# First key chunk ahead: the opening of an attention and SwiGLU kernel loaded and ordered anew

## The chip, the cores and the metric

The kernel runs on one core of one Trainium2 chip. The metric is the device time of one execution in microseconds (us), lower is better. The engines are called by the names that the profile uses: PE (TensorE, matrix products), ACT (ScalarE, functions), DVE (VectorE, elementwise work), POOL (GpSimd, here issues loads and copies) and SP (SyncE, issues DMAs). PEld is PE's loading of weights.

## The reference

Attention over 8 batches of 12 heads, 448 tokens and 64 dimensions, and behind it a gated feed-forward block (SwiGLU) over 3584 tokens, 768 wide inside and 1536 in the middle. All inputs come as float32.

```python
scores = scale * np.matmul(q, k.transpose(0, 1, 3, 2))      # q, k, v: 8, 12, 448, 64
attn = np.exp(scores - max); attn = attn / (sum(attn) + 1e-09)
x = np.matmul(attn, v)                                      # -> 3584 x 768
g = x @ w_gate
out = (g * sigmoid(g)) * (x @ w_val) @ w_out                # -> 3584 x 768
```

## The kernel before

The kernel works in fp16 with float32 accumulation. Heads are taken in pairs: pair 0 to 5 make batch 0, and there are 48 pairs in all. A pair's 448 keys are cut in four chunks (`NC`) of 112 (`P`). The work on a pair has these steps, and the letters are those of the order written out by hand in `OPENING`:

- **T** (`prep(pr)()`, function `turn`, lines 293 to 303): queries and keys of a pair are turned by 18 small matmuls against an identity (line 302) and copied by DVE (line 303) into `qkT`: columns 0 to 447 the keys, the rest the queries, the first 64 columns of them twice.
- **S** (`qk(pr, c)`, lines 353 to 367): two matmuls, one for each head, score a chunk of keys against all queries (line 359); ACT takes the exponential into `E` (line 367). The stationary operand has 128 columns, so it reads 16 columns of the next chunk along.
- **C** (`copy_v`, line 218): DVE copies the loaded values into a tile with a column of ones.
- **P** (`pv_chunk`, lines 377 to 411): eight matmuls (lines 385 and 393) multiply a chunk of exponentials with the values. After a pair's fourth chunk DVE divides by the sums (lines 404 and 406).
- **X** (`turn_x`, line 485): the pair's result is turned by three matmuls and DVE copies it (line 492) into `X`, the input of the feed-forward block.
- **D** (`dummy(1)`, line 163): one matmul of 512 columns on a tile of zeros, whose result nothing reads.

Each engine takes its instructions in the order in which the program emits them, so `OPENING` is the order of PE through the six pairs of batch 0, of ACT's exponentials, and of DVE's copies. After it a plan interleaves later pairs with the feed-forward steps; the first of them starts with the gate matmuls (`gp`, line 557) of batch 0, needs the X of pairs 0 to 4 at once and that of pair 5 a little later. In what follows S2.0 is chunk 0 of pair 2, and T6 the turn of pair 6.

Scores, turns and several later steps share a ring of three score buffers in PSUM (`ps_s`): a step that takes one waits until the work on the third one before it is done, an exponential for a score or a copy for a turn.

Loads: pair 0 is loaded by SP in float32 (`load_qk32`), one DMA for its queries and one for its keys. It is cast by DVE and ACT, one head each, turned by 16 matmuls (`turn0`, line 278) and copied by both (lines 286 to 289). All other pairs, the values and the weights are loaded by POOL's queue, which turns them to fp16 on the way (`load_qk16`, line 200; `load_v`, line 211; from pair 12 on also line 177). The first of these loads stand in a list before `OPENING`; later ones are emitted beside the second score chunk of a pair, from the table `wq`. From pair 11 on turns are done by POOL copies and DMA transposes issued by SP, no longer by PE.

Of the kernel before, what the change touches and what calls it, by code (L numbers as in the profile page):

```python
# [10 lines left out]
FP32 = mybir.dt.float32  # L11
FP16 = mybir.dt.float16
AF = mybir.ActivationFunctionType
# [5 lines left out]
GP = 3  # L19
NPE = 11  # L20
# [8 lines left out]
QB = 5  # L29
# [35 lines left out]
def kernel(  # L65
# [10 lines left out]
    nc = tc.nc  # L76
    B, H, S, D = q.shape
    DM = H * D
    DF = moe_w_gate.shape[1]
    P = 112  # L80
    NC = S // P
# [27 lines left out]
    attp = ctx.enter_context(tc.tile_pool(name="attp", bufs=4))  # L109
# [46 lines left out]
    raw = {}  # L156
# [3 lines left out]
    def dummy(n, w=4):  # L160
        wp = ps_f.tile([128, 512], FP32, tag="f", name="wp")
        for _ in range(n):
            nc.tensor.matmul(wp[:, 0 : w * 128], lhsT=warm[:], rhs=warm4[:, 0:w], start=True, stop=True)

    def load_qk32(pr):
        rq = fp.tile([P, 2, NC, D], FP32, tag="osb", bufs=4, name="rq")
        rk = fp.tile([P, 2, NC, D], FP32, tag="osb", bufs=4, name="rk")
        for dst, src in ((rq, q), (rk, k)):
            nc.sync.dma_start(dst[:], src[0, 2 * pr : 2 * pr + 2].rearrange("h (p c) d -> p h (c d)", c=NC))
        raw[pr] = (rq[:], rk[:])  # L170

    def load_keys(eng, dst, src, h0, n):
        for s in range(2):
# [12 lines left out]
    def load_qk16(pr, n=2):  # L186
        for t, src in ((0, q), (1, k)):
            if pr >= QUAD and t:
                if n == 1:
                    kd = rawslot(pr)[:, 1].rearrange("p (h x) -> p h x", h=2)  # L190
                else:
                    kd = raws_all[:, pr % RS // 2, 1].rearrange("p b (h x) -> p (b h) x", h=2)
                load_keys(nc.gpsimd, kd, k, 2 * pr, 2 * n)
                continue
            flat = src.rearrange("b h s d -> (b h) s d")[2 * pr : 2 * pr + 2 * n]
            if n == 1:
                dst = rawslot(pr)[0:P, t].rearrange("p (h x) -> p h x", h=2)
            else:
                dst = raws_all[0:P, pr % RS // 2, t].rearrange("p b (h x) -> p (b h) x", h=2)
            nc.gpsimd.dma_start(dst, flat.rearrange("h (p c) d -> p h (c d)", c=NC))  # L200
        for p in range(pr, pr + n):
            v4 = rawslot(p).rearrange("p t (h c d) -> p t h c d", h=2, c=NC)
            raw[p] = (v4[0:P, 0], v4[:, 1] if p >= QUAD else v4[0:P, 1])

    def load_v(pr, n=1):
        b, h = divmod(2 * pr, H)
        if pr >= QUAD:
            vd = vraw[:, ds(pr % VS, n)].rearrange("p r h c d -> p (r h) (c d)")
            load_keys(nc.gpsimd, vd, v, 2 * pr, 2 * n)
            return  # L210
        nc.gpsimd.dma_start(
            vraw[0:P, ds(pr % VS, n)].rearrange("p r h c d -> p (r h) (c d)"),
            v[b, h : h + 2 * n].rearrange("h (p c) d -> p h (c d)", c=NC),
        )
# [33 lines left out]
    def prep(pr):  # L248
        if pr >= QUAD:
            return prep_quad(pr)  # L250
        rq, rk = raw[pr]
        if pr == 0 or pr >= NPE:
            qk16 = attp.tile([128, 2, NC, 2, D], FP16, tag="qk16", name="qk16", bufs=3)[0:P]
            for t, src in enumerate((rq, rk)):
                dst = qk16[:, 1 - t].rearrange("p c h d -> p h c d")
                if pr == 0:
                    nc.vector.tensor_copy(dst[:, 0], src[:, 0])
                    nc.scalar.activation(dst[:, 1], src[:, 1], AF.Copy)
                else:
                    nc.gpsimd.tensor_copy(dst, src)  # L260
        qkT[pr] = attp.tile([128, 2 * S + D], FP16, tag="qkT", name="qkT", bufs=QB)
        if pr >= NPE:
            nc.sync.dma_start_transpose(
                qkT[pr][:, 0 : 2 * S].rearrange("p (c q) -> p c q", q=P),
                qk16.rearrange("p t c h d -> p (t c h d)"),
            )
            nc.sync.dma_start_transpose(
                qkT[pr][:, 2 * S :].rearrange("p (c q) -> p c q", c=1),
                qk16[0:D, 1, 0].rearrange("p h d -> p (h d)"),
            )  # L270
            return None

        def turn0():
            for t in range(2):
                tp = ps_s.tile([128, 2, 512], FP32, tag="s", name="tp")
                for c in range(NC):
                    for hx in range(2):
                        nc.tensor.matmul(
                            tp[ts(hx, 64), c // 2, ds(c % 2 * P, P)],
                            lhsT=qk16[:, 1 - t, c, hx],  # L280
                            rhs=ident[0:P, 0:P],
                            start=True,
                            stop=True,
                        )
                dst = qkT[pr][:, ts(1 - t, S)].rearrange("p (a x) -> p a x", a=2)
                copies = [nc.vector.tensor_copy(dst[:, 0], tp[:, 0, 0 : 2 * P])]
                if t == 0:
                    copies.append(nc.vector.tensor_copy(qkT[pr][:, 2 * S :], tp[:, 0, 0:D]))
                other = nc.scalar.activation(dst[:, 1], tp[:, 1, 0 : 2 * P], AF.Copy)
                for copy in copies:  # L290
                    tc.declare_no_dep(other.ins, copy.ins, reason="another bank, other columns")

        def turn():
            if pr < WIDE + 2:
                tp = ps_s.tile([128, 2, 1024], FP16, tag="s", name="tp")[:, 0]
            else:
                tp = ps_f.tile([128, 1024], FP16, tag="f", name="tp")
            for i in range(2 * NC + 1):
                t, c = (1 - i // NC, i % NC) if i < 2 * NC else (0, 0)
                for hx in range(2):  # L300
                    src = raw[pr][t][:, hx, c, :]
                    nc.tensor.transpose(tp[ts(hx, 64), ts(i, P)], src, ident[0:P, 0:P])  # L302
            nc.vector.tensor_copy(qkT[pr][:], tp[:, 0 : 2 * S + D])

        return turn if pr else turn0

    ering = []
    eslot = {}
# [44 lines left out]
    def qk(pr, c):  # L353
        if pr >= QUAD:
            return qk_quad(pr, c)
        t = qkT[pr]
        s = ps_s.tile([128, 2, 512], FP32, tag="s")
        for hx in range(2):
            nc.tensor.matmul(  # L359
                s[:, hx, 0:S],  # L360
                lhsT=t[ts(hx, 64), c * P : c * P + 128],
                rhs=t[ts(hx, 64), ds(S + (1 - hx) * D, S)],
                start=True,
                stop=True,
            )
        e = Es[pr % NE][:, ds(c * EB, 16)].rearrange("p (h b) x -> p h (b x)", h=2)
        nc.scalar.activation(e[:, :, 0:S], s[0:P, :, 0:S], AF.Exp, scale=sm_scale)  # L367
# [514 lines left out]
        return [(ch, m0, w) for m0 in range(0, DM, w) for ch in chunks]  # L882

    with tc.manual_schedule():
        load_qk32(0)
        nc.vector.memset(warm[:], 0.0)
        for e, eq in zip(Es, Eq):
            nc.vector.memset(eq[:, :, 2 * S :], 1.0)
# [3 lines left out]
            nc.vector.memset(vo[:, :, :, D:], 1.0)  # L892
        load_qk16(1, 1)
        make_identity(nc, ident)
        load_qk16(2, 1)
        load_v(0)
        load_qk16(3, 1)
        load_v(1)
        load_v(2)
        load_qk16(4)  # L900
        load_v(3, GP)
        dummy(7)
        dummy(1, 2)
        prep(0)()
        dummy(1)

        wq = {
            0: [("qk", 6), ("g", 0), ("v", 0)],
# [7 lines left out]
        def emit(item):  # L916
            if item[0] == "qk":
                load_qk16(*item[1:])
            elif item[0] == "V":
                load_v(item[1] * GP, GP)  # L920
            else:
                load_w(*item)
# [194 lines left out]
        def share(total, at, n):  # L1117
            return (at + 1) * total // n - at * total // n

        OPENING = """  # L1120
            S S D T D S S C D D S S D T S P P C P S C P
            S S P P T S P X P S S T C P S P P X S S P T C
            S P X P S S P P T S P P C S S X P P S S P X P T S P P S
        """.split()
        pieces = [(p, c) for p in range(FIRST) for c in range(NC)]
        nth = {kind: 0 for kind in "SCTXPD"}
        for kind in OPENING:
            n = nth[kind]
            nth[kind] += 1
            if kind == "S":  # L1130
                qk(*divmod(n, NC))
                if n % NC == 1:
                    for w in wq.pop(n // NC, []) if n < FIRST * NC else []:
                        emit(w)
            elif kind == "C":
                copy_v(n)
            elif kind == "T":
                prep(n + 1)()
            elif kind == "X":
                turn_x(n)  # L1140
            elif kind == "P":
                pv_chunk(*pieces[n])
            else:
                dummy(1)
# [304 lines left out]
```

## Time and profile before

| what | value |
| --- | --- |
| three runs | 429.09 to 429.46 us, median 429.46 us |
| the profiled execution | 428.9 us, its span 427.1 us, mean granted clock of PE 0.998 |
| PE busy | 419.8 us (98%) |
| ACT busy | 245.2 us (57%) |
| DVE busy | 269.6 us (63%) |
| POOL busy | 233.2 us (55%) |
| bytes moved by DMA | 50.02 MB, 117 GB/s on the mean |

The span runs from the first instruction to the last; some time lies around it, so the profiled execution's own time stands beside it. A matmul's end is modelled in the profile, so busy PE is not PE at its peak. Lines of the timeline give start and duration in us, engine, source line, operation, output<-input, the shape, a count, and in brackets the idle time before and what ended it.

### The profile page before, as it was taken

What the parts mean: (1) busy time and instruction counts of PE and PEld (TensorE: products, weight loads), DVE (VectorE), ACT (ScalarE), POOL (GpSimd) and SP (SyncE); (2) the same over time, 40 slices, a digit from 0 to 9 for tenths busy, and PEclk for the clock granted to TensorE, in tenths of its full rate; (3) what the DMA queues carried; (4) which work ended last, traced back from release to release, by engine and by line L of the source; (5) the groups of instructions that cost most, each with busy time, mean ns of one, the idle gap of its engine ahead of it and who ended that gap; (6) DMA issues with size and microseconds to landing.
All of it is one profiled execution on the core that took longest, in us unless ns stands there. A gap on an engine that the chain in (4) does not pass through costs nothing.

```text
span 427.1 us, 11621 instructions
## 1 busy us (share of the span) xinstructions
PE 419.8 (98%) x4636; PEld 290.1 (68%) x4636; DVE 269.6 (63%) x642; ACT 245.2 (57%) x395; POOL 233.2 (55%) x356
## 2 busy tenths in 40 slices
PE   8999999999999999999999999999999999999996
PEld 3666666555557777757666677777889985555795
DVE  4766562776669766575645776667777765665662
ACT  6976667546656655646666546559655235545221
POOL 8655634999697785538742784945999000000001
PEclk9999999999999999999999999999999999999999
DMA  9999999999999999999999997923100231000125
GB/s 133 190 200 200 200 176 188 135 156 225 132 149 130 129 191 124 141 114 138 118 148 111 152 142 108 142 56 100 23 1 22 93 109 41 0 0 2 38 76 148
DMA packets 108519, 50.02 MB, mean 117 GB/s; under 512 B 60832, under 2 KB 105200, under 8 KB 108464
## 3 DMA queue, kind: packets, MB, share of 16 engines
q0 software_dynamic: 46912, 24.83, 52.5%
q1 hardware_dynamic: 61408, 24.27, 33.9%
q8 instruction: 36, 0.59, 0.6%
q14 instruction: 19, 0.16, 0.2%
q10 hardware_dynamic: 144, 0.17, 0.1%
HBM read 49.55 MB, written 11.01 MB: 142 GB/s over the span
## 4 chain that ended last, share of the span: by engine, by line
PE 91%; DVE 3%; ACT 3%; DMA 1%; POOL 1%; issue 1%; SPq 0%; DVEq 0%; POOLq 0%
PE og L679 18%; PE gp L557 17%; PE vp L557 12%; PE un L795 10%; PE acc L420 8%; PE ub L795 8%; PE s L329 5%; PE op L650 3%; PE acc L385 2%; PE s L359 2%; DMA qkT<-qk 1%; ACT E L367 1%; PE s L341 1%; PE tp L302 1%; DVE t L610 1%; PE op L1001 1%
## 5 line engine op out<-in xcount | busy, mean ns | idle before, releaser
L349 ACT ACTIVATE E<-s 128x896 f16<-128x896 f32 x126 | 106.6, 918 | 40.2 <-PE s L329 28.2
L557 PE MATMUL gp<-X,wg 128*128 128x384 f16 (+1 forms) x360 | 73.9, 347 | 0.0
L237 POOL COPY qk<-qkraw 128x512 f16<-128x512 f16 x72 | 44.9, 667 | 51.3 <-DMA qkT<-qk 50.4
L557 PE MATMUL vp<-X,wv 128*128 128x384 f16 (+3 forms) x360 | 66.7, 321 | 0.1
L610 DVE SCALAR_TENSOR_TENSOR t<-sg,gp 128x384 f32<-128x384 f32 (+1 forms) x60 | 36.4, 608 | 41.5 <-ACT sg L584 41.2
L557 PEld LDWEIGHTS <-wv 128*128 128x128 f16 x462 | 43.7, 98 | 25.8 <-issue 0.3
L640 POOL DMA_DIRECT2D out_dram<-osb x3 | 1.6, 541 | 90.9 <-ACT osb L698 90.9
L557 PEld LDWEIGHTS <-wg 128*128 128x128 f16 x360 | 32.8, 98 | 26.3 <-issue 2.1
L177 POOL DMA_DIRECT2D vraw<-in_v_dram x72 | 43.8, 629 | 12.5 <-DVE X L492 7.3
L584 ACT ACTIVATE sg<-gp 128x384 f32<-128x384 f32 (+1 forms) x60 | 32.1, 537 | 28.2 <-PE gp L557 27.5
L177 POOL DMA_DIRECT2D qkraw<-in_k_dram x70 | 42.4, 619 | 7.2 <-DMA wo<-in_moe_w_out_dram 5.3
L367 ACT ACTIVATE E<-s 112x896 f16<-112x896 f32 x48 | 40.5, 918 | 7.8 <-PE s L359 7.8
L420 PEld LDWEIGHTS <-E 128*128 128x128 f16 (+1 forms) x1152 | 37.4, 96 | 11.2 <-issue 4.7
L679 PEld LDWEIGHTS <-hts 128*128 128x128 f16 x528 | 44.1, 98 | 0.3
L420 PE MATMUL acc<-vo,E 128*128 128x65 f16 (+1 forms) x1152 | 42.3, 192 | 1.0 <-DVE vo L218 0.3
L616 DVE SCALAR_TENSOR_TENSOR hts<-t,vp 128x384 f16<-128x384 f32 (+3 forms) x60 | 32.5, 541 | 5.5 <-PE vp L557 1.9
L698 ACT ACTIVATE osb<-og 128x384 f32<-128x384 f32 x22 | 10.8, 492 | 39.4 <-PE og L679 39.4
L450 DVE TENSOR_TENSOR xt<-acc,R 128x256 f16<-128x256 f32 x72 | 30.6, 425 | 2.5
L200 POOL DMA_DIRECT2D qkraw<-in_q_dram x43 | 29.3, 682 | 4.2 <-PE tp L302 1.1
L329 PE MATMUL s<-qkT 64*128 64x448 f16 x216 | 30.4, 354 | 0.2
L679 PE MATMUL og<-wo,hts 128*128 128x192 f16 x264 | 29.0, 246 | 0.0
L679 PEld LDWEIGHTS <-hsum 128*128 128x128 f16 x300 | 25.6, 98 | 1.0
(180 smaller groups left out, 724.9 us busy)
## 6 DMA issues: line engine op xcount, KB each, us to landing
vraw<-in_v_dram POOLq DMA_DIRECT2D x72, 64.0 KB, 4.6
qkraw<-in_q_dram POOLq DMA_DIRECT2D x39, 112.0 KB, 4.4
qkraw<-in_k_dram POOLq DMA_DIRECT2D x68, 64.0 KB, 4.7
wg<-in_moe_w_gate_dram POOLq DMA_DIRECT2D x8, 288.0 KB, 9.9
wv<-in_moe_w_val_dram POOLq DMA_DIRECT2D x8, 288.0 KB, 10.6
wo<-in_moe_w_out_dram POOLq DMA_DIRECT2D x2, 1152.0 KB, 19.1
out_dram<-osb SPq DMA_DIRECT2D x7, 288.0 KB, 3.7
out_dram<-osb SPq DMA_DIRECT2D x6, 336.0 KB, 3.0
```

Source lines behind the costliest of these rows:

```text
L177: eng.dma_start(dst[ts(s, 64)], rows)
L237: nc.gpsimd.tensor_copy(dst.rearrange("p c h d -> p h c d"), src)
L329: nc.tensor.matmul(s[:, hx, 0:S], lhsT=t[ts(hx, 64), ts(c + low(pr, hx), 128)], rhs=t[ts(hx, 64), ds(NC * 128, S)], start=True, stop=True,)
L349: nc.scalar.activation(e[:, 0 : 2 * S].rearrange("p (h q) -> p h q", h=2), s[:, :, 0:S], AF.Exp, scale=sm_scale)
L367: nc.scalar.activation(e[:, :, 0:S], s[0:P, :, 0:S], AF.Exp, scale=sm_scale)
L420: nc.tensor.matmul(acc[:, ts(j, D + 1)], lhsT=e[rows, ds(hx * S + j * 128, 128)], rhs=Vts[pr % NV][rows, hx, col, 0 : D + 1], start=first, ...
L557: nc.tensor.matmul(dst[:, 0:w], lhsT=wslice(kind, self.fb, cb), rhs=X[kk][:, cb, ds(c0 + lo, w)], start=(cb == 0), stop=(cb == NCB - 1),)
L584: self.readers = [nc.scalar.activation(self.sg[:, 0:n], gp[:, 0:n], AF.Tanh, scale=0.5)]
L610: nc.vector.scalar_tensor_tensor(self.t1[:, 0:n], self.sg[:, 0:n], 1.0, self.gp[:, 0:n], ALU.add, ALU.mult)
L616: nc.vector.scalar_tensor_tensor(self.hts[:, self.fb, ds(lo, w)], self.t1[:, ds(lo, w)], 0.5 * HS, vp[:, 0:w], ALU.mult, ALU.mult)
L679: nc.tensor.matmul(dst, lhsT=lhs(n), rhs=rhs(n), start=first and n == 0, stop=n == NH - 1, skip_group_check=True)
L795: mm = nc.tensor.matmul(dst, lhsT=lhs[:, n], rhs=rhs[:, n], start=first and n == 0, stop=n == NK - 1, skip_group_check=True,)
```

## The change

Four things are changed, all at the beginning of the program.

- The keys of pair 0 come in two loads instead of one: first the first 64 of each line of 256 elements (chunk 0), then the other three chunks. The queries are loaded ahead of both, as before.
- `first_turns` takes the place of `turn0`. Queries and key chunk 0 are cast, turned and copied; ACT, which copied the upper half of the keys, now copies key chunk 0 (112 columns). The other three chunks are cast then, and a new step **K** in `OPENING` turns them by six matmuls and has DVE copy them in two pieces. The score of chunk 0 of pair 0 takes a stationary operand of 112 columns, so it does not read chunk 1.
- Loads on POOL's queue: queries and keys of pairs 2 and 3 are loaded as one pair of DMAs instead of two, and the values of pairs 0, 1 and 2 as one DMA instead of three; they follow behind the keys of pair 3, where value 0 was ahead of pair 3 before.
- `OPENING` is another order of the same S, C, T, P and X, with K added and two D in place of five. The matmuls on zeros ahead of the opening are 6 of 512 columns and one of 384, instead of 7 and one of 256.

```diff
-    def load_qk32(pr):
+    def load_first():
         rq = fp.tile([P, 2, NC, D], FP32, tag="osb", bufs=4, name="rq")
-        rk = fp.tile([P, 2, NC, D], FP32, tag="osb", bufs=4, name="rk")
-        for dst, src in ((rq, q), (rk, k)):
-            nc.sync.dma_start(dst[:], src[0, 2 * pr : 2 * pr + 2].rearrange("h (p c) d -> p h (c d)", c=NC))
-        raw[pr] = (rq[:], rk[:])
+        rk = [fp.tile([P, 2, n, D], FP32, tag="osb", bufs=4, name="rk") for n in (1, NC - 1)]
+        qs, ks = (src[0, 0:2].rearrange("h (p c) d -> p h (c d)", c=NC) for src in (q, k))
+        for dst, src in ((rq, qs), (rk[0], ks[:, :, 0:D]), (rk[1], ks[:, :, D:])):
+            nc.sync.dma_start(dst[:].rearrange("p h c d -> p h (c d)"), src)
+        return rq, rk
...
+    def first_turns(rq, rk):
...
+        nc.vector.tensor_copy(q16[:, 0], rq[:, 0])
+        nc.scalar.activation(q16[:, 1], rq[:, 1], AF.Copy)
+        nc.vector.tensor_copy(k16[:, :, 0:1], rk[0][:])
+        for c in range(NC):
+            turned(tq[:, c // 2, ds(c % 2 * P, P)], qk16[:, 1, c])
+        turned(tk[:, 0, 0:P], qk16[:, 0, 0])
+        dst = t[:, ts(1, S)].rearrange("p (a x) -> p a x", a=2)
+        low = nc.vector.tensor_copy(dst[:, 0], tq[:, 0, 0 : 2 * P])
+        high = nc.scalar.activation(dst[:, 1], tq[:, 1, 0 : 2 * P], AF.Copy)
+        again = nc.vector.tensor_copy(t[:, 2 * S :], tq[:, 0, 0:D])
+        key = nc.scalar.activation(t[:, 0:P], tk[:, 0, 0:P], AF.Copy)
...
+        nc.scalar.activation(k16[:, 1, 1:], rk[1][:, 1], AF.Copy)
+        nc.vector.tensor_copy(k16[:, 0, 1:], rk[1][:, 0])
+        dummy(1)
+
+        def others():
+            for c in range(1, NC):
+                turned(tk[:, 1, ts(c - 1, P)], qk16[:, 0, c])
+            for lo, n in ((1, 1), (2, 2)):
+                nc.vector.tensor_copy(t[:, ds(lo * P, n * P)], tk[:, 1, ds((lo - 1) * P, n * P)])
...
         t = qkT[pr]
+        w = 128 if pr or c else P
         s = ps_s.tile([128, 2, 512], FP32, tag="s")
...
-                s[:, hx, 0:S],
-                lhsT=t[ts(hx, 64), c * P : c * P + 128],
+                s[0:w, hx, 0:S],
+                lhsT=t[ts(hx, 64), c * P : c * P + w],
...
-        load_qk16(2, 1)
-        load_v(0)
-        load_qk16(3, 1)
-        load_v(1)
-        load_v(2)
+        load_qk16(2)
+        load_v(0, GP)
         load_qk16(4)
         load_v(3, GP)
-        dummy(7)
-        dummy(1, 2)
-        prep(0)()
-        dummy(1)
+        dummy(6)
+        dummy(1, 3)
+        other_keys = first_turns(*first)
...
-            S S D T D S S C D D S S D T S P P C P S C P
-            S S P P T S P X P S S T C P S P P X S S P T C
-            S P X P S S P P T S P P C S S X P P S S P X P T S P P S
+            S K S S D T D S S S S T S C C S T S P P S S P P P P C P S T
+            S X P C S S C P P P X S S P P P T S X P S S C P P P P P S X
+            S S X T P P P S P S T
```

## The prediction

> **What bounds the kernel now.** I read the page first: busy times, then the chain that ended last.
>
> ```profile
> PE 419.8 (98%) x4636; PEld 290.1 (68%) x4636; DVE 269.6 (63%) x642; ACT 245.2 (57%) x395; POOL 233.2 (55%) x356
> ...
> PE 91%; DVE 3%; ACT 3%; DMA 1%; POOL 1%; issue 1%; SPq 0%; DVEq 0%; POOLq 0%
> ```
>
> TensorE (PE) carries the span: a microsecond taken from PE's order anywhere is taken from the end, unless a later wait gives it back. So I ask when PE leaves the opening (first gate matmul, at 27.16 us), and where it waits afterwards. First the timeline of the opening (start, duration, engine, line, operation):
>
> ```profile
> 3.81 0.42 ACT L258 ACTIVATE qk<-rq 112x256 f16<-112x256 f32 x1 [1.79 <-DMA rq<-in_q_dram]
> ...
> 4.31 1.28 PE L278 MATMUL tp<-ident,qk 112*64 112x112 f16 x16
> ...
> 5.62 0.39 DVE L286 CAST qkT<-tp 128x224 f16<-128x224 f32 x1 [0.16 <-PE tp L278]
> ...
> 6.07 0.55 PE L359 MATMUL s<-qkT 64*128 64x448 f16 x4
> 6.47 15.83 ACT L367 ACTIVATE E<-s 112x896 f16<-112x896 f32 x19 [0.50 <-PE s L359]
> ...
> 12.52 0.55 PE L359 MATMUL s<-qkT 64*128 64x448 f16 x4
> ...
> 13.01 0.36 PE L385 MATMUL acc<-vo,E 112*128 112x65 f16 x6
> ...
> 13.26 0.34 PE L385 MATMUL acc<-vo,E 112*128 112x65 f16 x6
> ...
> 13.59 0.63 PE L302 MATMUL tp<-ident,qkraw 112*64 112x112 f16 x18
> ...
> 14.16 0.36 PE L359 MATMUL s<-qkT 64*128 64x448 f16 x2
> ```
>
> ScalarE (ACT) runs exponentials from 6.47 without a pause (the next start 0.80 to 0.81 us after the last when nothing is late, 0.918 each), and PE is just as full. From start to start in this timeline, a step of PE costs: a score chunk (S) 0.20 before another, 0.29 before anything else; a product chunk (P) 0.25 before another, 0.34 before a score or a turn; a turn (T) 0.57; a turn of X 0.17 to 0.26; a filler (D) 0.23 to 0.32. Over the order of before these give 20.2 us; from the first score at 6.07 to 27.16 are 21.1, so PE waited 0.9 in all, nearly all of it before 11.05, where the products begin. Both engines bind.
>
> Then the DMA, by windows (us; busy PE, PEld, DVE, ACT, POOL; granted clock; DMA share; GB/s):
>
> ```profile
> 4.50:10.00 5.50, 5.27 (x55) 2.22 (x53) 2.22 (x6) 4.64 (x8) 5.50 (x9) 1.00 1.16 138
> 10.00:12.50 2.50, 2.33 (x54) 1.78 (x53) 1.38 (x3) 2.50 (x4) 2.50 (x5) 1.00 1.28 156
> 12.50:17.50 5.00, 5.00 (x112) 3.53 (x110) 3.52 (x8) 5.00 (x7) 2.79 (x4) 1.00 1.42 192
> ```
>
> While single pairs are loaded, one issue per 0.66 us on POOL for 115 KB, the rate is 138 GB/s; with the larger loads it is 192, and it stays near 200 until 75 us. There, after 27.16, is the one place where PE waits long: the timeline of DVE, then of PE.
>
> ```profile
> 76.08 0.46 DVE L218 COPY vo<-vraw 128x512 f16<-128x512 f16 x1 [1.84 <-DMA vraw<-in_v_dram]
> 76.46 0.55 DVE L492 CAST X<-xtp 128x384 f16<-128x384 f32 x1
> ```
>
> ```profile
> 76.59 0.20 PE L420 MATMUL acc<-vo,E 64*128 64x65 f16 x1 [0.31 <-DVE vo L218]
> 77.05 0.72 PE L420 MATMUL acc<-vo,E 64*128 64x65 f16 x18 [0.26 <-DVE X L492]
> ```
>
> The values of pair 12 land late (DVE idles 1.84 us for them), and PE, which would have gone on 0.29 after its last score (75.92), starts at 76.59 and again at 77.05: 0.37 and 0.43 us lost. At 83.27 a score takes 0.49 to its successor instead of 0.20, released by a DMA transpose that lands at 83.72: 0.29 more. Together 1.1 us, by the DMA's clock, not PE's.
>
> **The change, part by part.** The sum is against the profiled execution, 428.9 us (span 427.1 and 1.8 around it), 0.56 below the median of 429.46.
>
> *Start.* Query casts and turns stay (4.31 to 4.89). One key chunk (64 KB instead of 229) cannot land before the queries (3.79) and, by the row of the whole keys, not after 4.51; at either end its cast, turn (0.09) and copy fit beside the query copies, which on DVE end at 5.46. So the first score goes at 5.52 instead of 6.07. SP's third issue (0.45) delays nobody; the remaining chunks land by 4.5 to 5.2 (the end of the keys now, or one more step of 0.72), and ACT is free for their cast only at 5.4, behind the copy of the key chunk. Cast 0.30 to 0.42 (row: 0.42 for 256 columns, here 192), so until 5.74.
>
> *K.* Six more matmuls at 5.8, results at 6.1 (as the last turn of line 302 takes 0.21), then two DVE copies, 112 and 224 columns: 0.27 (between the rows 0.21 for 64 and 0.39 for 224) and 0.39, overlapping by 0.08, to 6.73. The second score chunk reads 128 columns from 112, 16 of them in the second copy, so it waits for both: 6.79, exponential at 7.20. Before it was 7.29. So of the 0.55 gained by the first, 0.09 is left at the second; ACT idles about 0.4 between.
>
> *The order.* From there ACT sets the pace: the products come only after score 10, since the merged values land later than value 0 alone did. Scores are let in by the three score buffers as exponentials end. The seventh (pair 1, chunk 2) starts at 7.20 + 5 x 0.806 = 11.23 and ends at 12.15; its buffer lets in pair 2's first score at 12.2. Behind that stand 52 steps before the gate matmuls: 18 scores 4.74, 24 products 6.66, 5 turns 2.83, 5 turns of X 1.12: 15.4 us. None waits by my count but T6 (0.1 for its buffer). Gate at 12.2 + 15.4 + 0.1 = 27.7, **0.55 later** than 27.16. The new order saves 1.0 us of switching and fillers (19.2 for 20.2), but PE idles some 3 us before 12.2. Lower bound: were only ACT binding, the 24th exponential would start at 7.20 + 22 x 0.806 = 24.93; its end, the last product (0.06 later), one score and T7, now behind it, give 24.93 + 0.92 + 0.06 + 0.34 + 0.28 + 0.57 = 27.1, 0.06 earlier. Upper bound: K 0.3 later (its casts a DMA step later), 28.0. I take 27.7: it is the sum of rows that PE showed itself to follow.
>
> *Fillers.* Three fewer in the opening, in the sums already; 6.75 instead of 7.5 before it, where PE waits for the queries anyway (4.31). What they cover is the clock (rivals).
>
> *Loads.* Seven issues become three: four times 0.66 us of POOL, its next issues 2.6 us earlier, and the DMA has 229 KB and more per issue at once. If the 4.1 us from 5.9 and the 2.5 us from 10 went at 192 GB/s, all later loads would land (54 x 4.1 + 36 x 2.5) / 192 = 1.6 us earlier; with no better rate, 0. I take 1.2, nearer the rate that the same packets show from 12.5. Values 0 to 2 stand behind the keys of pair 3 now: 0.80 MB after pair 1 (6.26) at 192 GB/s is 10.4, at 138 it is 12.1 (before: 9.08, 11.31, 11.92); their copies come up on DVE at 12, with the copy of T3 queued behind, so 0.1 at most. No weight is waited for before or after. But values 12 and the transposes land earlier by as much, the queue being full until 75 us and POOL paced by landings; 0.6 is enough to pass PE's own arrival. The three waits go: **1.1 us back** (0 if no load is earlier).
>
> Sum: +0.55 - 1.1 = -0.55. 428.35 for the profiled execution, **428.9** as a median. The opening only shifts the rest: PE has no other wait there that is not on its own chain.
>
> **Rivals.** (0.2% is 0.86 us, about what a measurement of this kernel can tell from no change.)
>
> *B: ACT alone binds.* PE catches up and the gate comes at 27.1. For: ACT had no pause after 6.47. Against: PE's steps add up almost exactly in before. -0.06 - 1.1 = -1.2: 428.3.
>
> *C: loads no earlier*, if the rate of 138 belongs to the size of the packets (512 bytes in both) and not to the issues. Then landings stay, PE arrives 0.55 later and waits that much less: the transpose at 83.72 releases it as before. 0: 429.5. Against: the same packets went at 192 from 12.5.
>
> *D: the clock falls back, slower.* The clock of PE is judged in stretches of 3.41 us: full speed was granted at 5.69 and withdrawn at 425.53, 123 stretches apart; rows:
>
> ```profile
> 422.11:425.53 3.42, 0.76 (x10) 0.53 (x7) 0.36 (x1) 0.49 (x1) 0.72 (x2) 1.00 0.69 205
> 425.53:427.10 1.57, 0.00 (x0) 0.00 (x0) 0.00 (x0) 0.00 (x0) 0.00 (x0) 0.50 0.01 2
> 75.00:78.41 3.41, 2.84 (x56) 1.76 (x54) 0.92 (x2) 3.00 (x4) 3.41 (x7) 1.00 0.84 118
> ```
>
> A stretch 22% busy lost it, one 83% busy kept it. In the new order 9.1 to 12.5 holds about four scores (0.36) and a turn (0.63): 60%. If the point lies above that, 3.41 us at half speed do 1.7 us of work less, right where PE binds: +0.55 + 1.7 - 1.1 = +1.15, 430.6. The distance from 60% to either row leaves it open; waits of half a microsecond are nearer the kept one. The Trainium skill, TensorE: Matmul & The Clock Gate, section "A second HAM failure mode: psum-queue depth-cycling", says that short idling between groups of matmuls while PSUM buffers cycle can make the clock oscillate, which would be this case; its "Why this matters" asks only for no gaps over about 3 us, which would not. No row here decides between the two.
>
> *E: the first chunk gains nothing*, its pieces being 256 bytes in place of 1024, and K comes 0.5 later: +1.0 - 1.1 = -0.1, 429.4.
>
> **Numbers.** Forecast 0.46 (own range 428.3 to 429.8: opening +0.2 to +0.85, relief 0.8 to 1.1, widened by 0.3 for the spread of the runs, 429.09 to 429.46); B 0.17, C 0.13, D 0.17, E 0.07. Faster by over 0.2%: 0.18 of the forecast and B, 0.35. Slower: D's 0.16, and 0.02 each of forecast, C and E, 0.22. Same 0.43. The range goes from B with all the relief (1.5 under the median) to D: 427.9 to 430.6.
>
> **What would show it.** First exponential at 5.9, second at 7.2; pair 2's first score at 12.2; products from 13.4; gate at 27.7; PE's clock full throughout; pair 12's values landing before 75.4; the lines at 76.59 and 77.05 without a wait, and no jump at 83.3. Wrong if the gate comes before 27.2, if loads at 17 us land no earlier than now (value 3: 17.36), or if matmuls slow to half between 9 and 16 us.

## The result, and the profile after

The changed kernel takes **462.98 us** (median of four runs, 462.75 to 463.99); the kernel before took 429.27 beside it (429.03 to 429.46). The ratio is 1.0781, with an interval from 1.0760 to 1.0803: 33.7 us lost, where the prediction had 0.6 gained. The profiled execution took 463.19 us, its span is 461.4, and the mean granted clock of PE is 0.954 in place of 0.998. From the page, in its order: busy times, the clock in 40 slices of 11.5 us, the chain that ended last, and one group:

```profile
PE 424.3 (92%) x4632; PEld 292.9 (63%) x4632; DVE 267.1 (58%) x644; ACT 245.4 (53%) x395; POOL 229.9 (50%) x352
...
PEclk8665599999999999999999999999999999999999
...
PE 78%; DMA 10%; POOL 5%; DVE 3%; ACT 2%; issue 2%; DVEq 0%; POOLq 0%; ACTq 0%
...
L278 PE MATMUL tp<-ident,qkraw 112*64 112x112 f16 x180 | 7.6, 240 | 28.1 <-DMA qkraw<-in_k_dram 27.8
```

PE was busy 98% of the span and is busy 92%, with only 4.5 us more work: it waits. The last line names the wait: of the 28.1 us that PE idled ahead of the turns (line 278 here), 27.8 ended with a load of keys. The timeline of PE shows that it is a single wait:

```profile
23.98 0.22 PE L411 MATMUL acc<-vo,E 112*128 112x65 f16 x2
52.00 1.05 PE L278 MATMUL tp<-ident,qkraw 112*64 112x112 f16 x18 [27.80 <-DMA qkraw<-in_k_dram]
```

Which load this is, the timeline of POOL tells. Of the loads of keys, the last that POOL issued ahead of 52.00 is this one, and the trace lets it land at 51.86:

```profile
42.37 0.61 POOL L178 DMA_DIRECT2D qkraw<-in_k_dram  x1 [0.88 <-DMA wv<-in_moe_w_val_dram]
```

Line 178 loads pairs from 12 on: it is the load of pairs 12 and 13. Raw queries and keys have eight slots, and a pair takes the slot of its number modulo 8, so pair 13 goes into the slot of pair 5. This load is emitted by the entry `4: [..., ("qk", 12)]` of `wq`, beside S4.1. In the order of before T5 stands ahead of S4.0, so it reads pair 5 and the load waits for T5. In the new order T5 stands *behind* S4.1. The load is now the earlier of the two in the program, and T5 waits for it. (In the changed kernel, then, T5 turns the block of pair 13 in place of that of pair 5, and pair 5's scores are made from it; that much of the computation is changed.)

The second loss is the clock. Windows of the changed kernel, cut where the granted clock may change (us; busy time and count of PE, PEld, DVE, ACT, POOL; granted clock; DMA share; GB/s):

```profile
5.62:9.03 3.41, 2.00 (x32) 0.90 (x30) 0.93 (x3) 2.14 (x4) 3.41 (x5) 1.00 1.19 138
9.03:12.44 3.41, 2.90 (x25) 1.30 (x23) 0.66 (x1) 3.03 (x4) 1.55 (x3) 0.50 1.36 176
12.44:15.86 3.42, 3.15 (x40) 1.65 (x36) 1.60 (x4) 2.85 (x5) 2.31 (x3) 0.50 1.45 196
15.86:19.27 3.41, 3.41 (x52) 2.59 (x51) 0.70 (x3) 2.59 (x3) 1.32 (x2) 0.50 1.40 200
```

After a stretch in which PE was busy 2.00 of 3.41 us (59%), three follow at half speed. The idle time of that stretch is two waits, 0.67 us for the cast of the other key chunks and 0.74 for the copies of K. The clock is lost again during the long wait, from 26.1 to 56.8. Nor did the opening start as forecast. Its timeline of ACT:

```profile
6.16 0.36 ACT L312 ACTIVATE qk<-rk 112x192 f16<-112x192 f32 x1 [0.79 <-DMA rk<-in_k_dram]
6.42 0.90 ACT L385 ACTIVATE E<-s 112x896 f16<-112x896 f32 x1
8.05 1.73 ACT L385 ACTIVATE E<-s 112x896 f16<-112x896 f32 x2 [0.73 <-PE s L377]
10.16 4.27 ACT L385 ACTIVATE E<-s 112x896 f16<-112x896 f32 x5 [0.38 <-PE s L377]
```

The first exponential stands behind the cast of the other key chunks (line 312), and that waits for their load, which landed at 6.13. So the first score, though early (5.43), bought nothing: 6.42 for 6.47 before. The rest of the program is only shifted. Matched matmul by matmul, PE runs 34.4 us behind at the gate matmuls (61.56 for 27.16) and 33.1 behind past the places where the kernel before had waited for values 12 and the transposes (76 to 84 us there).

### The profile page after: what moved, and what is told of

Its sections match the earlier page's. It is cut to its first block, busy times and chain, and to the rows that moved or that the text cites. A ratio compares the mean times of both kernels' runs of the same rounds, so it can differ in the third digit from the quotient of the medians.

```text
span 461.4 us, 11616 instructions
## 1 busy us (share of the span) xinstructions
PE 424.3 (92%) x4632; PEld 292.9 (63%) x4632; DVE 267.1 (58%) x644; ACT 245.4 (53%) x395; POOL 229.9 (50%) x352
## 4 chain that ended last, share of the span: by engine, by line
PE 78%; DMA 10%; POOL 5%; DVE 3%; ACT 2%; issue 2%; DVEq 0%; POOLq 0%; ACTq 0%
PE og L697 16%; PE gp L575 16%; PE vp L575 11%; PE acc L438 7%; PE un L813 7%; PE ub L813 5%; PE s L346 5%; PE op L668 4%; DMA wv<-in_moe_w_val_dram 4%; DMA qkraw<-in_k_dram 3%; DMA wg<-in_moe_w_gate_dram 3%; PE acc L403 2%; PE s L377 1%; PE s L358 1%; DVE t L628 1%
## 5 line engine op out<-in xcount | busy, mean ns | idle before, releaser
L366 ACT ACTIVATE E<-s 128x896 f16<-128x896 f32 x126 | 106.6, 918 | 40.2 <-PE s L346 28.2
L238 POOL COPY qk<-qkraw 128x512 f16<-128x512 f16 x72 | 43.8, 653 | 87.2 <-DMA qkT<-qk 81.3
L602 ACT ACTIVATE sg<-gp 128x384 f32<-128x384 f32 (+1 forms) x60 | 32.1, 537 | 28.4 <-PE gp L575 27.7
L278 PE MATMUL tp<-ident,qkraw 112*64 112x112 f16 x180 | 7.6, 240 | 28.1 <-DMA qkraw<-in_k_dram 27.8
```

What stands on the lines that cost most here:

```text
L238: nc.gpsimd.tensor_copy(dst.rearrange("p c h d -> p h c d"), src)
L366: nc.scalar.activation(e[:, 0 : 2 * S].rearrange("p (h q) -> p h q", h=2), s[:, :, 0:S], AF.Exp, scale=sm_scale)
L602: self.readers = [nc.scalar.activation(self.sg[:, 0:n], gp[:, 0:n], AF.Tanh, scale=0.5)]
```

## The experiments

### Where the 33.7 us went: the slot and the clock

**e1_load_behind_t5** and **e2_before_t5_late**: take the slot wait away from the changed kernel, and put it alone into the kernel before.

```diff
 e1, the changed kernel:
-            4: [("g", 3), ("v", 3), ("qk", 12)],
+            4: [("g", 3), ("v", 3)],
+            5: [("qk", 12)],
 e2, the kernel before (T5 moved from behind P2.3 to behind S4.1; it turns pair 13's block there too):
-            S S P P T S P X P S S T C P S P P X S S P T C
-            S P X P S S P P T S P P C S S X P P S S P X P T S P P S
+            S S P P T S P X P S S T C P S P P X S S P C
+            S P X P S T S P P T S P P C S S X P P S S P X P T S P P S
```

> The changed kernel with one edit: the load of pairs 12 and 13 is emitted beside score S5.1 instead of S4.1, so behind T5 (in the changed kernel T5 stands behind that load in the program, and reads the block that it fills; here it reads pair 5's own again). Theory, slot: T5 waited 27.8 us because that load, which takes pair 5's buffer, is emitted ahead of it. Then the wait is gone, the clock stays as it was up to 19.3 us and isn't lost again at 26.1: gate at 61.56 - 27.8 - 2.4 = 31.4 us, 1.1 back at 76 to 84 us: 432.4 us. Rival, queue: pair 5's own block lands late because loads were merged; then the wait stays, about 463. Rival, clock: the 41 us at half clock are the loss and the wait is only its shadow; then the clock record stays as it is and the time stays over 445.

> The kernel before with one edit: T5 moved in the order from ahead of S4.0 to behind S4.1, and so behind the emission of the load of pairs 12 and 13 (T5 then turns that block in place of pair 5's). Theory, slot: T5 waits for that load, which landed at 52.5 us in the profile of before; PE, due at T5 at about 20.5, idles some 31 us, loses the clock and pays 2 to 3 us for it: about 429.3 + 31 + 2.5 - 1.1 = 461.5 us. Rival, queue: nothing is merged here, so about 429.3. Rival, clock: PE is as busy as before up to T5, so 429.3.

e1 took 434.32 us (ratio 1.0111, 1.0096 to 1.0126), so one table entry is worth 28.7 of the 33.7. e2 took 462.58 (1.0766, 1.0743 to 1.0788), and its waits of PE begin with

```profile
PE tp L302 <- DMA qkraw<-in_k_dram: 32.3, 1, 32.3
```

(in total, times, longest). The misplaced turn alone makes the kernel before as slow as the changed one. But e1 stayed 1.9 above what was expected, 1.2 of it at the gate (32.6 for 31.4), and its timeline of PE says why:

```profile
7.73 0.93 PE L377 MATMUL s<-qkT 64*128 64x448 f16 x4 [0.74 <-DVE qkT L320]
8.59 0.61 PE L163 MATMUL wp<-warm 128*128 128x512 f16 x1
```

These steps take 0.55 and 0.39 at full clock. In this execution the clock was not lost but never granted before 20.09; windows show 1.00 up to the first grant, and the mean clock doesn't count that time, so only the durations tell.

**e3_fillers**: e1 with eight fillers more in the first half of the opening, where PE idles.

```diff
-            S K S S D T D S S S S T S C C S T S P P S S P P P P C P S T
+            S D D K D D S S D T D S D S D S D S D T D S C C S T S P P S S P P P P C P S T
```

> The first experiment's kernel with eight more fillers in the order: two on either side of K, and one each between the scores S0.3 to S1.3, where PE only waits for buffers. Theory, clock second: the half clock from 9.03 to 19.27 us is lost PE time, about 3 us of it on the path; with PE kept busy from 5.6 to 9.0 the granted clock stays full, the gate comes at about 28.6 us (second exponential at 8.05 because the other key chunks land at 6.1) and the time is 429.3 + 1.4 - 1.1 = 429.6 us, 2.8 less than the first experiment. Rival: the opening is bound by ACT and by landings, the clock costs nothing; then the time is that of the first experiment, within 0.4.

431.23 us (1.0035, 1.0020 to 1.0050): full clock from 6.31 on, the gate at 29.1 in place of 32.6 in e1. The clock was worth 3.1 us, net of what the fillers cost. Two kernels without any fillers in `OPENING` ask whether fillers are what holds it:

**e7_no_fillers**: the kernel before, its five D of `OPENING` left out. **e14_order_no_fillers**: the kernel before with the changed order (without K, pairs 12 and 13 loaded behind T5), no D in it.

> The kernel before without the five fillers of the opening. Theory, clock: they hide in waits of PE and cost nothing, and without them PE is about 65% busy from 5.7 to 9.1 us, which is between the changed kernel's 59% that lost the clock and the 83% that kept it; if lost, PE runs at half speed for one stretch or more from 9.1 us, the gate comes 2 to 4 us later, and the time is 430.5 to 433. Rival, fillers are mere delay: gate at 27.1, the time is 429.5 or less.

> The kernel before with the change's order (without K, keys of pairs 12 and 13 behind T5) and with no filler in the opening at all (the order with its one filler gave 429.35, ratio 0.9997). Theory (fillers are dead weight where ACT sets the pace, the clock is held by the turns and scores): gate 27.4 to 27.8, 428.9 to 429.4. Rival (the clock needs them, stretches below 62 % lose it): a stretch of 57 to 62 % between 7 and 14 loses the clock, gate 29.5 to 31, 431.5 to 433.

e7: 429.12 us (0.9985, 0.9975 to 0.9996), **the fastest kernel of this study**, 0.15% below the kernel before. The clock theory missed: in the profile the stretches after the first grant are busy 2.71 and 2.11 of 3.41 us, and the clock stayed.

```profile
3.73:7.14 3.41, 2.71 (x44) 1.30 (x42) 1.72 (x6) 2.33 (x6) 3.41 (x6) 1.00 1.10 115
7.14:10.56 3.42, 2.11 (x28) 1.13 (x27) 1.28 (x3) 3.42 (x5) 3.42 (x6) 1.00 1.22 155
10.56:13.97 3.41, 3.41 (x76) 2.40 (x74) 2.03 (x6) 3.41 (x5) 3.20 (x5) 1.00 1.32 168
```

e14: 429.69 (1.0005, 0.9994 to 1.0016); a stretch with 2.05 of 3.41 (60%) kept the clock in its profile.

```profile
5.52:8.93 3.41, 2.05 (x27) 1.08 (x27) 1.03 (x2) 2.91 (x5) 3.41 (x6) 1.00 1.12 130
```

So 60% busy does not by itself lose the clock, and the median gains nothing from the fillers. But they are not without effect. One stretch at half speed takes 0.004 from an execution's mean clock. Five of the twelve executions of e14 have 0.991 or 0.996, and two of e7 have 0.994 and 0.996; none of 129 executions of the kernel before is under 0.997. Without fillers, then, the clock seems to be lost in some executions (no profile shows one of them), and it costs little: those of e14 at 0.991 took 429.95 to 430.59 us, those at 1.0 took 429.07 to 430.16.

**e12_mended_whole**: the change with its two wrong inputs repaired (pairs 12 and 13 behind T5; pair 0's keys in one load of 224 KB, `first_turns` taking its two parts from it), and no filler added to the order of the change.

> This is the change with two repairs and nothing else: the keys of pairs 12 and 13 emitted behind T5 instead of ahead of it, and pair 0's keys in one load; the order is the change's own, with no fillers added (the run before it, with eight fillers more, had its first exponential at 5.92, its second at 7.83 because two fillers of 0.60 stood ahead of K, its gate at 28.4 and a median of 430.79). Theory (the prediction's sum holds once its two wrong inputs are mended, and the fillers are dead weight): first exponential 5.9, second 7.2 to 7.3, gate 27.7 to 27.9, clock kept, 430.0 to 430.4. Rival (the fillers hold the clock): the stretches from about 5.6 to 16 are 60 to 66 % busy in this order and the clock is lost there, as it was in the change: gate 30 to 32, 432.5 to 434.5.

Median 430.68 (1.0044, 1.0024 to 1.0064), but from 429.59 to 433.75: four executions (430.55 to 432.44) show a mean clock of 0.991 to 0.994, the two longest one of 0.998 and 1.0. The profiled execution, 432.34, shows the second exponential at 7.32, as the theory had it, and then (timeline of PE)

```profile
11.86 1.05 PE L278 MATMUL tp<-ident,qkraw 112*64 112x112 f16 x18 [1.51 <-DMA qkraw<-in_k_dram]
```

T2 waits for the merged keys of pairs 2 and 3, which landed at 11.82 here, the stretch is 46% busy, and the turn runs at half clock (1.05 for 0.63). **e13_separate_loads** takes only the merging away from e12:

```diff
-        load_qk16(2)
-        load_v(0, GP)
+        load_qk16(2, 1)
+        load_v(0)
+        load_qk16(3, 1)
+        load_v(1)
+        load_v(2)
```

> The mended change (keys of pairs 12 and 13 behind T5, pair 0's keys in one load, the change's own order) with the loads of pairs 2 and 3 and of the values 0 to 2 apart again. Theory (the merged load starves the opening: pair 2's turn waits for pair 3's bytes): no wait of T2 for its load, second exponential 7.3, pair 2's first score at 12.2 or earlier, gate 27.0 to 27.7, clock kept in all its runs, 429.0 to 429.7. Rival (the first-chunk code is what costs, by its two stalls of 0.33 and by what it does to the weights of the output): gate as in the theory, but 430.0 to 430.8 at the end.

Missed by both: median 432.05 (1.0054, 1.0028 to 1.0079), in two groups of six executions, 429.31 to 430.98 and 433.12 to 434.15, all with a mean clock of 0.995 to 1.0. T2 waits for no load any more, so the merging was not what spreads the times. The profiled execution, 430.84, lost the clock for one stretch, behind one that was 62% busy:

```profile
8.72:12.13 3.41, 2.12 (x29) 1.08 (x28) 1.00 (x3) 3.41 (x5) 3.41 (x5) 1.00 1.30 164
12.13:15.55 3.42, 3.42 (x42) 2.08 (x42) 1.09 (x3) 2.71 (x4) 2.34 (x4) 0.50 1.31 165
```

Two more profiled executions of the same kernel are **e15_look_a** and **e15_look_b**, below called a and b:

> The kernel of e13_separate_loads once more, for its profile alone. Theory (late first grant): a profiled run near 433.5 has no full clock until 12 or later, one near 429.8 has it from about 5.3; gate some 3 us apart. Rival (something after the opening, a weight or a transpose late): the gate comes at 29.0 in both and a jump follows at 73 to 84.

> The same kernel and the same two readings as in the look before it: a late first grant with the gate some 3 us later, or a gate at 29.0 and a jump at 73 to 84.

They took 433.83 and 429.61 us. The same two steps as in e1, on PE's timelines, first a, then b:

```profile
7.33 0.93 PE L377 MATMUL s<-qkT 64*128 64x448 f16 x4 [0.74 <-DVE qkT L320]
8.19 0.61 PE L163 MATMUL wp<-warm 128*128 128x512 f16 x1
```

```profile
7.01 0.55 PE L377 MATMUL s<-qkT 64*128 64x448 f16 x4 [0.75 <-DVE qkT L320]
7.50 0.39 PE L163 MATMUL wp<-warm 128*128 128x512 f16 x1
```

One kernel, two executions: a is not granted the clock until 20.42, b has it at 5.22. The gate is 4.5 us apart (32.55 and 28.00), the end 4.2. Their times fall into the two groups of e13, so the groups are most likely executions whose clock is granted at once, or late; only these two were profiled to tell. The stretches of 3.41 us lie differently in each execution. In b one of them, 1.81 to 5.22, fell on the fillers ahead of the opening and was 93% busy. In a they lay 1.5 us later, so the first that could have granted it already holds a part of the pause behind K:

```profile
3.36:6.77 3.41, 3.07 (x21) 1.09 (x19) 1.36 (x6) 1.85 (x5) 3.41 (x7) 1.00 1.14 137
6.77:10.18 3.41, 2.85 (x24) 1.17 (x24) 0.86 (x3) 2.08 (x3) 3.41 (x6) 1.00 1.23 148
10.18:13.60 3.42, 2.91 (x27) 1.53 (x26) 0.31 (x1) 2.75 (x4) 3.42 (x5) 1.00 1.26 157
13.60:17.01 3.41, 3.15 (x38) 1.78 (x37) 1.72 (x4) 2.84 (x4) 2.00 (x4) 1.00 1.43 191
```

90, 83, 85 and 92% busy at half speed, and none was enough (1.00 stands for "no grant yet"). The Trainium skill, TensorE: Matmul & The Clock Gate, Part 1, says the window of 3413 ns is free-running and does not start with the kernel; a and b agree, with stretches that begin 3.36 and 1.81 us after the first instruction.

**e16_fillers_behind_k**: e13 with four fillers where PE idles.

```diff
-            S K S S D T D S S S S T S C C S T S P P S S P P P P C P S T
+            S K D D S S D T D S S S D S D T S C C S T S P P S S P P P P C P S T
```

> The kernel of e13_separate_loads with four fillers more: two behind K, where PE idles 0.75 us, one ahead of a score that waits 0.32 for its buffer, one ahead of the turn that waits 0.44. Theory (late or lost clock is what spreads e13): all runs in one group, second exponential still 7.3, gate 27.0 to 27.5, 429.2 to 429.9. Rival (the groups come from elsewhere): two groups as before, median 430.5 to 432.

One group, 429.47 to 431.52, and the first two exponentials are those of the prediction (timeline of ACT):

```profile
5.82 0.92 ACT L385 ACTIVATE E<-s 112x896 f16<-112x896 f32 x1 [0.24 <-PE s L377]
7.20 12.37 ACT L385 ACTIVATE E<-s 112x896 f16<-112x896 f32 x15 [0.46 <-PE s L377]
```

But the median is 430.65 (1.0021, 1.0010 to 1.0032), and the gate 28.2: the theory on the groups held, the time it gave did not. In the profiled execution, the longest of the twelve, 1.6 us more are lost behind the gate: 0.3 comes back at 76 us, 0.5 goes at a transpose that lands late (83.8), 0.7 by 131 us, and twice some 0.35, below.

### The first chunk

**e5_first_chunk**: the kernel before with the split load, `first_turns` and K alone (and four D around K); **e9_whole_keys**: e5 with pair 0's keys in one load; **e11_change_mended**: e3 with the same.

```diff
-        rk = [fp.tile([P, 2, n, D], FP32, tag="osb", bufs=4, name="rk") for n in (1, NC - 1)]
+        rk = fp.tile([P, 2, NC, D], FP32, tag="osb", bufs=4, name="rk")
...
-        for dst, src in ((rq, qs), (rk[0], ks[:, :, 0:D]), (rk[1], ks[:, :, D:])):
+        for dst, src in ((rq, qs), (rk, ks)):
...
-        return rq, rk
+        return rq, (rk[:, :, 0:1], rk[:, :, 1:])
```

> The kernel before with only the first key chunk taken apart: its load, first_turns and K as in the change, K behind S0.0, with two fillers on either side of K so that PE stays busy; loads and order otherwise as before. Theory, late chunks: the first exponential comes at 6.3 to 6.5 and the second at 8.0 to 8.4, since the other three chunks land at about 6.1, behind the loads of pair 1, instead of 4.5 with the whole keys; against 7.29 before that is 0.8 to 1.1 later, the gate as much later, and at 76 to 84 us all but 0.2 is given back: gate 28.1, time 429.7 us, same. Rival, as the prediction had it: second exponential at 7.2, gate at 27.1, time 429.4.

> The fifth experiment's kernel (first chunk taken apart, old loads and order, fillers around K) with the keys of pair 0 loaded by one DMA again, and only cast, turned and scored by chunk. Theory, split load: the three other chunks come at 4.5 us instead of 6.7, so their cast on ACT no longer holds up the first exponential: first at 5.9 to 6.1, second at 7.2 to 7.4, gate at 27.1, time 429.4, some 1.6 less than the fifth experiment. Rival, K itself: the extra turns and copies are what delays; the second exponential stays at 8 or later and the time at 431.

> The whole change (merged loads, new order, first chunk ahead) with three mends: the load of pairs 12 and 13 behind T5, the fillers of the third experiment, and the keys of pair 0 in one load. Theory: second exponential at 7.2 to 7.4 instead of 8.39, gate at 28.0 instead of 29.1, and the stage at 76 to 84 us gives most of the rest back: 430.0 us. Rival, the split load does not matter under this order, since PE waits for other things: 431.2 as in the third experiment.

e5 took 431.02 us (1.0033, 1.0019 to 1.0047): the step that was to help costs 1.4 by itself. Its timeline of ACT:

```profile
6.76 0.36 ACT L312 ACTIVATE qk<-rk 112x192 f16<-112x192 f32 x1 [1.31 <-DMA rk<-in_k_dram]
7.03 0.90 ACT L385 ACTIVATE E<-s 112x896 f16<-112x896 f32 x1
8.65 0.92 ACT L385 ACTIVATE E<-s 112x896 f16<-112x896 f32 x1 [0.73 <-PE s L377]
```

The other chunks landed at 6.73. With one load for all keys (landed 4.37) e9 takes 430.24 (1.0016, 1.0003 to 1.0029) and e11 430.79 (1.0024, 1.0009 to 1.0039; e3, with the split load, 431.23). In e11 ACT begins

```profile
5.92 0.92 ACT L385 ACTIVATE E<-s 112x896 f16<-112x896 f32 x1 [0.24 <-PE s L377]
7.83 6.77 ACT L385 ACTIVATE E<-s 112x896 f16<-112x896 f32 x8 [1.00 <-PE s L377]
```

so the first exponential is 0.55 earlier, but the two D ahead of K hold K up and the second comes at 7.83. Both stayed above the expected time. Part of that is a thing with no name yet: in the profile of every kernel that has `first_turns`, PE falls 0.3 to 0.4 us further behind at the same score of the later program (165.8 us in the kernel before) and again at 327.2; no kernel without it does. At the first place the timeline of PE shows 0.14 to 0.16 us of idling that ends with a DVE step (`osb`, line 753), at the second 0.27 that ends with a POOL step (`hsum`, line 560), in a with a DVE step (`un`); the kernels without `first_turns` show no idling there. Releasers are inferred, and the second differs between two executions of one kernel, so the cause stays open; together it is 0.7 us in each of these kernels.

### The order and the loads by themselves

**e6_new_order**: the kernel before with the changed order, without K, pairs 12 and 13 loaded behind T5. **e4_merged_loads**: the kernel before with the merged loads alone (the diff of e13, the other way).

> The kernel before with only the order of the opening as in the change (without K, and with the load of pairs 12 and 13 behind T5, so that T5 turns pair 5); start and loads as before. Theory, order and clock: PE is only some 60% busy from 9.1 to 12.5 us, the products begin at 13.4; with the clock full the gate comes at 27.7 us, 0.6 later, and the stage at 76 to 84 us gives it back: 429.5. If the stretch of 3.41 us in which scores stand alone loses the clock, the gate comes 1.7 to 3 later still, 29.4 to 30.7, and the time is 430.6 to 432. Rival: the order is better with the old loads, since the values land from 9 us: gate at 27.1 or before.

> The kernel before with only the loads of pairs 2, 3 and of values 0 to 2 merged, the order of the opening as before. Theory: values 0 land at 12.2 us instead of 9.1, and the copy C0 stands on DVE ahead of the copy of T2, so that score S1.2 comes about 2 us later; later loads land about 1 us earlier, which gives back the 1.1 us at 76 to 84: 429.3 + 2.0 - 1.1 = 430.2 us. Rival, issue-bound loads (as the prediction had it): loads from the fifth on land 1.2 us or more earlier at 17 us and the time falls below 429. Rival, packet-bound: value 3 lands at 17.4 as before, nothing is given back: 431.3.

e6: 429.35 us (0.9997, 0.9982 to 1.0012), gate at 27.82, clock kept in its profile: by itself the order changes nothing that these runs can tell. e4: 430.29 (1.0019, 1.0004 to 1.0035). Its PE waits for the merged values:

```profile
12.95 0.34 PE L385 MATMUL acc<-vo,E 112*128 112x65 f16 x6 [1.56 <-DVE vo L218]
```

and the loads behind it are earlier by about half of what was forecast: the values of pair 3 land at 16.67, for 17.36 in the kernel before. One pair of profiles says little here, since without merging they land at 16.70 in e6 and at 16.34, 16.95 and 17.17 in three executions of one kernel (a, b, e13). Over all profiles they land at 15.65 to 17.64 in the six with merged loads and at 16.34 to 17.92 in the other thirteen, with medians of 16.5 and 17.2. By 76 us nothing of this is left: the values of pair 12 land at 77.26 in e4, for 75.98 in the kernel before.

### The relief behind the gate

**e8_late_weights**: the kernel before, ("o", 1), a half of the output weights, emitted beside pair 9 in place of pair 8. **e10_values12_early**: e7 with the values of pair 12 emitted beside pair 8, ahead of where they stood.

```diff
 e8:
-            8: [("o", 1)],
+            9: [("o", 1)],
 e10:
-                    if 12 <= pr + 3 < NPAIR:
+                    if pr == 8:
+                        load_v(12)
+                    if 12 < pr + 3 < NPAIR:
```

> The kernel before with the load of the second half of the output weights (1.15 MB) emitted beside pair 9 instead of pair 8, behind the values of pair 12 and the queries and keys of pair 15. Theory, DMA-timed stage: values 12 land 2 us or more earlier than 75.99, so that PE's waits at 76.6 and 77.05 go, and perhaps that for the transposes at 83.7; time 0.7 to 1.1 lower, 428.5 us. Rival: the weights, then landing after 75, are waited for at 78.4 (their first use), or PE's chain binds there anyway: 429.5 or more.

> The seventh experiment's kernel (before without fillers) with the values of pair 12 loaded beside pair 8, ahead of the second half of the output weights, instead of beside pair 9. Theory, DMA-timed stage: values 12 land before 75 us, so the waits at 76.6 and 77.05 go (0.8); the weights land some 0.7 later than 73.1 and are waited for at 73.2. Net 0.1 to 0.3 less than the seventh experiment, 428.9. Rival: as in the eighth experiment the clock falls back at the new wait and the time is over 430.

e8 missed: 433.35 us (1.0092, 1.0075 to 1.0110). The weights themselves came late, and the clock was lost from 76.89 to 80.30 behind the wait (timeline of PE):

```profile
76.94 3.38 PE L650 MATMUL op<-wo,hts 128*128 128x384 f16 x10 [3.76 <-DMA wo<-in_moe_w_out_dram]
```

e10 missed too: 429.84 (1.0007, 0.9993 to 1.0021). The waits for values 12 went, and what then stood in the way (waits of PE: in total, times, longest) was

```profile
PE s L341 <- DMA qkT<-qk: 0.9, 1, 0.9
...
PE op L650 <- DMA wo<-in_moe_w_out_dram: 0.8, 1, 0.8
```

a transpose and the output weights. Values and weights stand in one queue, POOL's, and in the profile of before DMA moves 176 to 200 GB/s from 10.7 to 74.7 us, so one load is made earlier by making another late.

## Why the prediction was wrong, step by step

- **The order** ("5 turns 2.83 ... None waits by my count but T6"). This is the step that failed, by 28.7 us (462.98 to 434.32 in e1). PE's steps, the score buffers and the exponentials were counted through the order, but not the DMAs that the order emits: `wq` hangs its loads on score chunks, and T5 was moved past S4.1 and so past a load into its own slot. "No weight is waited for" looked at loads as things to wait for, not as things that overwrite. e1 and e2 show it from both sides.
- **The clock** (rival D, 0.17). That it falls was right; where, why and how long were not. "9.1 to 12.5 holds ... 60%" was one stretch too late: 5.62 to 9.03 was 59% busy and lost it. What PE waited for in it were the late key chunks and K, not score buffers. And not 3.41 us but three stretches went at half speed, because the first two of them were 85 and 92% busy and that did not bring it back. It is worth 3.1 us (e1 to e3), and 4.2 between a and b, where the clock was granted late and not lost. Of the two rules that the prediction cites from the Trainium skill, TensorE: Matmul & The Clock Gate, that of "A second HAM failure mode: psum-queue depth-cycling" (short idling is enough) is nearer to this row, though PSUM buffers were not what PE waited for; by "Why this matters for your kernels", which asks for no gaps over about 3 us, the clock would have stayed: the longest gap in the stretch that lost it was 0.74 us. But the rows between are not ordered by busy time: 59% (changed kernel) and 62% (e13, 2.12 of 3.41) lost it, 60% (e14) and 62% (e7) kept it. What else decides is open.
- **The start** ("first score at 5.52"; "the remaining chunks land by 4.5 to 5.2"). The first held (5.43; the chunk is 57 KB, not 64); the second was 0.9 us past its later bound in the changed kernel (6.13) and 1.5 in e5 (6.73). The bounds came from the row of the whole keys, lines of 1024 bytes; the rest of the lines has 768, and in the trace its packets went out from 3.0 to 5.7 between those of pair 1's loads. The first exponential on ACT waits behind their cast. With one load for all keys the steps are as predicted: first exponential 5.82 to 5.94, second 7.20 to 7.32 (e16, e12), against "5.9" and "7.2".
- **The pace** ("12.2", "27.7"). Right where the clock holds: pair 2's first score at 12.27 and gate at 28.00 in b, and the gate at 27.82 in e6 (both with the old loads). The 15.4 us for 52 steps were 15.7.
- **The fillers** cost nothing in the opening as assumed, save the two ahead of K in e11, but for "Three fewer" the cover was gone: with `first_turns` and no more of them, six of twelve executions fall into the longer group (e13), which a puts down to the late grant; in the kernel before all five can go without a loss of time (e7).
- **The loads** ("I take 1.2"). Too much: the values of pair 3 land 0.7 us earlier (16.67 in e4 for 17.36; 0.7 between the medians of all profiles), and by 76 us, where the gain was to come, nothing is left (values 12 at 77.26 for 75.98), as rival C had it. The merged ones land later for whoever needs their first part (values 0 at 12.6 in e4 for 9.1).
- **The relief** ("1.1 us back"). The size was near, the cause wrong. In the changed kernel and in e1 PE's lag behind the kernel before falls by 1.3 us from the gate to 84 us, in b by 0.84. These are waits for DMA at a fixed time, and a PE that comes late doesn't wait there. So the near size was luck. It is no gain: it gives back what the opening lost, up to 1.3 us here. In e10, where the values came early, it was not got.
- **The sum.** With the slot and the load mended and the clock granted, b says what the forecast should have been: +0.84 at the gate, -0.84 by 77 us, +0.39 and +0.38 at the two unnamed stalls; 429.61 for the profiled 428.9 of before. What is left of the change in such an execution is a loss of 0.7 to 0.8 us.

Of the 33.7 us, then, 28.7 are the slot (to e1: the wait of 27.8 and the clock lost in it), 3.1 the clock in the opening (to e3), 0.4 the split load (e3 to e11, no more than the spread of either). The last 1.2 to 1.5 (430.79 against 429.27 to 429.59) are in parts the fillers ahead of K, the merged loads (0.8 alone, e4) and the unnamed stalls; these don't add up singly, since the waits at 76 to 84 us swallow what the opening loses.

## What to carry to other kernels

When steps of a hand-written order are moved, list every load emitted along the way with the slot that it overwrites, and check for each moved reader on which side of that load it now stands; a turn moved by two score chunks cost 28.7 us here. Price a gain in the opening only after asking whether a later wait has a fixed time, because such a wait gives back a loss and eats a gain. And look at the spread of the executions, not only at the median and one profile: two groups with equal mean clock were one kernel, and in the two profiled executions the first grant came early or late.

## What the runs showed of the hardware

- Busy time alone decides neither the grant nor the loss of the clock. At half speed, stretches of the opening 77 to 92% busy did not bring it (a, e1, e12, the changed kernel), those 100% busy did. But ahead of the opening, where only the fillers of 512 columns run, a stretch 90% busy brought the first grant in e2 (0.66 to 4.07) and one 80% busy in e7 (0.32 to 3.73, 2.74 of 3.41 us). At full speed, stretches with 60 to 69% kept it in six profiles (e4, e6, e7, e10, e14, b), 46, 59 and 62% lost it in three (e12, the changed kernel, e13). Whether it matters which matmuls fill a stretch is not tested.
- The record of the granted clock is silent before the first grant: a ran at half speed until 20.42 us and shows a mean of 0.998.
- Splitting a load of 1024-byte lines into 256 and 768, beside POOL's loads, brought the first part forward and put the second back: they land at 3.65 to 3.82 and at 6.06 to 6.73 us in the four profiles with it, the whole load at 4.19 to 4.59 in the fifteen without.
